# A build-time scheduler gets a longer latency for small transfers behind weight loads, and two margins

## The chip, the cores and the metric

One core of one Trainium2 chip. The metric is device time in microseconds (us), the median of several executions of the same program on the same data. Executions of one kernel agree here within 0.1% mostly. All runs told below are in the fast state, at a granted TensorE clock of 1.0 (0.999 in a few). Engines: PE is TensorE, ACT ScalarE, DVE VectorE, POOL GpSimd, SP the engine that issues nearly all transfers. "The profile" is a hardware trace of one execution; its span is about 2 us shorter than the time (690.4 and 692.2 for the profiled execution of the kernel before).

## The reference, cut to what matters

```python
x = A_x                                   # [1, 2048, 512] bf16
xn = _layernorm(x)
return x + _A_ref(xn, A_wqkv, A_wo) + _B_ref(xn, B_w1, B_b1, B_w2, B_b2)

def _A_ref(x, wqkv, wo):                  # attention, 32 heads of 16, softmax over 2048 keys
    ...
    scores = jnp.einsum("bhqd,bhkd->bhqk", q, k) * scale
    p = _softmax(scores, axis=-1)
    o = jnp.einsum("bhqk,bhkd->bhqd", p, v)
    return ... @ wo

def _B_ref(x, w1, b1, w2, b2):            # a second layernorm, then an MLP over the 2048 tokens
    u = _gelu(jnp.einsum("bsd,sf->bdf", h, w1) + b1)      # F = 1376
    y = jnp.einsum("bdf,fs->bds", u, w2) + b2
```

The bulk is 32 x 2048 x 2048 exponentials. The kernel cuts them into 1024 tiles of 128 x 1024.

## The kernel before

It is one program with the order of every engine's instructions fixed at build time. A Python scheduler, inside the kernel file, keeps a clock for each engine, looks at what could be done next, and greedily appends the candidate with the earliest estimated time. Nothing at run time follows this clock: the chip keeps each engine's order and waits on semaphores. The time of a transfer in it:

```python
if op.is_dma:
    op.t0 = max(self.free[eng], ready)
    self.free[eng] = op.t0 + cost[0]      # DMA_I = 0.65: SP's issue
    op.t1 = op.t0 + cost[1]               # DMA_L = 3.0: landed
```

A candidate's estimate adds a slack of `DMA_SLACK = 0.8` us for each operand that a transfer writes. The slack only delays the moment at which the candidate is chosen; it is not in the clock.

```python
def est(specs, slack=0.0):
    for s_ in specs:
        r = max(r, sc.ready(s_["eng"], s_["reads"], s_["writes"], slack=slack, dma_slack=DMA_SLACK))
```

An exponential tile goes to ScalarE as one instruction, or to VectorE as one (`dexp`), followed by three shifted copies by VectorE or GpSimd. The first costs PE one group of four PV matmuls (softmax weights times V), the second four groups. Which engine takes a tile is the scheduler's choice, so the split (715 to 309 before) is a result of the order.

After each of the 32 blocks of heads the denominators go around by transfers, all issued by SP, and meet again in VectorE:

```python
for c in range(4):   # dcomp <- OT32      4 small transfers
...                  # oC32  <- OT32      8 small transfers
yield "dve", [... e.reciprocal(rcomp[:, eb, :], dcomp[:, eb, :]) ...]
...                  # rden_scratch <- rcomp
for r in range(4):   # denb <- rden_scratch   4 small transfers
...
for h in range(2):   # the products, for each second block
    yield "dve", [... e.tensor_tensor(oT(qb)[0:m, T, cs], oC32[...], denb[...], ALU.mult) ...]
```

The MLP runs in PE's gaps: eleven first-layer tiles, each with a 512 KB load of `w1` (the last 384 KB), then sixteen output tiles, each with a 320 KB load of `w2` and two small ones. These loads stand in SP's order among the small transfers above.

The softmax here doesn't subtract the row's maximum and nothing guards it: scores larger than these inputs give would overflow.

Of the kernel before, what the change touches and what calls it, by code (L numbers as in the profile page):

```python
# [28 lines left out]
NBLK = NQB * NG  # L29
NN = NBLK * NKT * 2  # L30
# [22 lines left out]
SEM = 0.05  # L53
PE_SWITCH = 0.10
PER_LIST = 16
LN2_AT = 12
PIECE_MIN = 6
PIECE_OPEN = 1
HOLD_MAX = 2.0
PE_LAT = 0.40  # L60
# [5 lines left out]
DMA_I = 0.65  # L66
DMA_L = 3.0
DMA_SLACK = 0.8
EXT_SLACK = 0.2
PV_SLACK = 0.1  # L70
GEN_SLACK = 0.0
# [2 lines left out]
OT_I, OT_L = 0.60, 0.685  # L74
D_END = 1022
D_FLY = 3
D_BACK = 0.5
D_STEAL = 0.3
D_LATE = 0.5
P_KEEP = 4  # L80
DEAD_SLACK = 0.1
PAIR_WAIT = 0.0
PORT_SLACK = 0.5
PE_FIT = 0.05
TABLE = 1.3
# [2 lines left out]
Q_GUARD = 8  # L88
KV_LEAD = 16
HARD_HOLD = 10  # L90
LATE_BY = 0
EX_FROM = 34
EX_RATE = 0.15
EX_EARLY = 10
# [28 lines left out]
class Sched:  # L123
    ENGS = ("pe", "act", "dve", "pool", "sp")

    def __init__(self, nc, es):
        self.nc = nc
        self.es = es
        self.streams = {e: [] for e in self.ENGS}
        self.order = []  # L130
        self.last_writer = {}
        self.readers = {}
        self.dma_ops = []
        self.free = {e: 0.0 for e in self.ENGS}
        self.busy = {e: 0.0 for e in self.ENGS}
        self.pe_mode = None
        self.pe_end = 0.0
        self.pe_tiles = {}
        self.phase = 0
        self.pieces = {}  # L140
        self.pe_log = []
        self.port_iv = {"dve": [], "pool": []}
        self.port_op = None

    def _deps(self, eng, reads, writes, dma):
        deps = set()
# [36 lines left out]
    def _time(self, op, cost, ready, port):  # L183
        eng = op.eng
        if port:
            ready = self.port_time(eng, max(self.free[eng], ready), cost[0])
        if op.is_dma:
            op.t0 = max(self.free[eng], ready)
            self.free[eng] = op.t0 + cost[0]
            op.t1 = op.t0 + cost[1]  # L190
        elif eng == "pe":
            mode, tiles, dur = cost
            t = max(self.free["pe"], ready)
            if mode != self.pe_mode:
                t = max(t, self.pe_end + PE_SWITCH)
                self.pe_mode = mode
                self.pe_tiles = {}
                self.phase += 1
            for x in tiles:
                t = max(t, self.pe_tiles.get(x, 0.0))  # L200
            for x in tiles:
                self.pe_tiles[x] = t + dur
            self.pe_end = max(self.pe_end, t + dur)
            self.free["pe"] = t + 0.004
            self.busy["pe"] += dur * len(tiles) / 4.0
            op.t0, op.t1 = t, t + dur + PE_LAT - 0.214
            self.pe_log.append((t, dur * len(tiles) / 4.0))
        else:
            op.t0 = max(self.free[eng], ready)
            self.free[eng] = op.t0 + cost[0]  # L210
            self.busy[eng] += cost[0]
            op.t1 = op.t0 + cost[1]
        if port:
            self.port_iv[eng] = self.port_iv[eng][-7:] + [(op.t0, op.t0 + cost[0])]
# [124 lines left out]
def bass_parallel_sum__softmax_full_mha__mixer_token_mlp__prompt_kernel(  # L339
# [18 lines left out]
    with ExitStack() as es:  # L358
# [31 lines left out]
        dcomp = sb("dcomp", [128, 2, 16], F32)  # L390
# [8 lines left out]
        def oT_keys(qb, T):  # L399
            return [("oTc", qb, T)] + (WKV_KEYS if qb >= 2 else [])  # L400
# [622 lines left out]
        def task_epilogue(b):  # L1023
            p, e_ = divmod(b, 2)
            qb, T = PAIRS[p]
            eb, tb_ = b % 2, p % 2
            yield "gate", lambda: b < 2 or b - 2 in ot_free
            yield "pvev", [dict(eng="dve", fn=lambda e: e.tensor_copy(OT32[:, eb, :], bank(PV_BANK)),  # L1028
                                reads=[("bank", PV_BANK)], writes=[("OT32", eb)])]
            for c in range(4):  # L1030
                yield "sp", [dict(dst=dcomp[32 * c:32 * c + 32, eb, :],
                                  src=OT32[32 * c + 16:32 * c + 17, eb, :].rearrange("o (c x) -> o c x", x=16),
                                  reads=[("OT32", eb)], writes=[("dcomp", eb, c)], name="den_in")]
            g_in = dict(gen=task_o_in(b), cur=None)
            if b == NBLK - 2:
                yield "call", lambda: (step_gen(g_in), frees.append(g_in))
            else:
                yield from task_o_in(b)
            yield "dve", [dict(eng="dve", fn=lambda e: e.reciprocal(rcomp[:, eb, :], dcomp[:, eb, :]),
                               reads=[("dcomp", eb, r) for r in range(4)], writes=[("rcomp", eb)], cost=(0.2, 0.25))]  # L1040
            yield "sp", [dict(dst=rden_d[eb].rearrange("(p x) -> p x", x=16), src=rcomp[:, eb, :],
                              reads=[("rcomp", eb)], writes=[("rden_d", eb)], name="den_mid")]
            for r in range(4):
                a, i = divmod(r, 2)
                ro = 64 * e_ + 16 * r
                src = rden_d[eb:eb + 1, :].rearrange("o (h i a x) -> o h i a x", h=2, i=2, a=2)[:, :, i, a, :]
                yield "sp", [dict(dst=denb[ro:ro + 16, tb_, :].rearrange("p (h x) -> p h x", h=2),
                                  src=src.to_broadcast([16, 2, 256]),
                                  reads=[("rden_d", eb)], writes=[("denb", tb_, e_, r)], name="den_out")]
            half = b == NBLK - 2  # L1050
            if e_ == 0 and not half:
                return
            es_ = (0,) if half else (0, 1)
            m = 64 if half else 128
            if half:
                yield "call", lambda: sc.add("dve", lambda e: e.memset(oT(qb)[64:128, T, :], 0.0),
                                             writes=oT_keys(qb, T), cost=(0.2, 0.26))
            yield "gate", lambda: b in ot_free and (half or b - 1 in ot_free)
            for h in range(2):
                cs = slice(256 * h, 256 * h + 256)  # L1060
                yield "dve", [dict(eng="dve", fn=lambda e, cs=cs: e.tensor_tensor(  # L1061
                    oT(qb)[0:m, T, cs], oC32[0:m, tb_, cs], denb[0:m, tb_, cs], ALU.mult),
                    reads=[("oC32", tb_, x, c, a) for x in es_ for c in range(4) for a in range(2)] +
                          [("denb", tb_, x, r) for x in es_ for r in range(4)],
                    writes=oT_keys(qb, T) + [("oTh", h)], port=True, cost=(0.33, 0.41))]
            yield "call", lambda: oT_done.add((qb, T))

        oT_done = set()
# [200 lines left out]
        def est(specs, slack=0.0):  # L1269
            s0 = specs[0]  # L1270
            r = 0.0
            for s_ in specs:
                r = max(r, sc.ready(s_["eng"], s_["reads"], s_["writes"], slack=slack, dma_slack=DMA_SLACK))
            t = max(sc.free[s0["eng"]], r)
            if s0.get("port"):
                t = sc.port_time(s0["eng"], t, s0["cost"][0])
            return t
# [24 lines left out]
        def pieces():  # L1302
# [12 lines left out]
            for tries in range(2):  # L1315
                for o in list(g["open"]):
                    for r in sorted(o[1]):
                        if piece_phase[1] not in (None, r) or max(sc.free["pe"], sc.pe_tiles.get(r, 0.0), sc.piece_ready(r)) + 0.214 > lim:
                            continue
                        sp_ = o[0](r, not g.get("begun"), hold and g["stop"] and len(g["open"]) == 1 and len(o[1]) == 1)  # L1320
                        if est(sp_) > sc.free["pe"] + 0.02:
                            continue
                        if not g.get("begun"):
                            g["begun"] = True
                            g["cur"] = ("pe", g["front"](False))
                        piece_phase[1] = r
                        for z in sp_:
                            add(z)
                        o[1].discard(r)
                        if not o[1]:  # L1330
                            g["open"].remove(o)
                        if hold and not g["open"]:
                            g.pop("since", None)
                            step_gen(g)
                            return
                        break
                if len(g["steps"]) >= PIECE_MIN and len(g["open"]) < PIECE_OPEN and g["steps"][-1][1]:
                    g["open"].append((g["steps"].pop(-1)[1], {0, 1, 2, 3}))
                else:
                    return  # L1340
# [22 lines left out]
        step_gen(g_h)  # L1363
        fin_next = 0
        while True:
            cands = []

            for g in sorted(frees, key=lambda g: not (g["cur"] and g["cur"][0] == "sp" and g["cur"][1][0]["name"] == "q_row")):
# [289 lines left out]
```

## Time and profile before

| | before |
|---|---|
| time, median of 4 | 691.96 us (691.90 to 692.06) |
| span of the profile | 690.4 us |
| exponential tiles on ScalarE / VectorE | 715 / 309 |
| last exponential on ScalarE ends at | 681.88 us |
| last PV matmul ends at | 682.22 us |

The busy shares, the waits and the rows of the groups are shown in the prediction. Timelines (columns): start, duration, engine, line, operation, tiles, form, count, and in brackets the idle time before and what ended it.

```profile
677.03 4.84 ACT L768 ACTIVATE pT<-ps 128x1024 bf16<-128x1024 f32 x5
687.32 0.60 ACT L1127 ACTIVATE oT<-ps 128x512 bf16<-128x512 f32 x1 [5.44 <-PE ps L1107]
...
666.33 0.82 PE L842 MATMUL ps<-gT_sb,wblk 128*32 128x512 bf16 x12
...
681.48 0.74 PE L811 MATMUL ps<-pT,V 128*32 128x256 bf16 x16
682.16 0.60 PE L1107 MATMUL ps<-wo_c,wkv_raw 128*128 128x512 bf16 x2
```

The exponentials end at 681.9 us, the PV matmuls 0.3 us later, and then comes a closing part (last denominators, last output rows) of 8.2 us, in which ScalarE sits idle for 5.44 us.

### The profile page before, as it was taken

The numbers are of one execution on the slowest core, as the hardware profiler recorded it, in microseconds if no ns is written. First come the engines' busy times: TensorE is split into PE (matmuls) and PEld (weight loads), VectorE is DVE, ScalarE is ACT, GpSimd is POOL, SyncE is SP. The second block draws the span as 40 slices with busy tenths as digits, with TensorE's granted clock in tenths as the row PEclk, the third lists the DMA queues.
The fourth block names the chain that finished last, engine by engine and source line by source line (L and its number), as shares of the span: only waits on it lengthen the run. The fifth ranks groups of instructions, "written<-read, shape, count | busy, mean of one in ns | idle before, by whom it ended". The sixth has DMA issues, their size and how long they took to land.

```text
span 690.4 us, 29398 instructions
## 1 busy us (share of the span) xinstructions
PE 674.3 (98%) x12934; PEld 309.7 (45%) x12934; DVE 618.7 (90%) x895; ACT 672.3 (97%) x734; POOL 401.7 (58%) x690
## 2 busy tenths in 40 slices
PE   7999999999999999999999999999999999999998
PEld 4534544435444454444444444444444444444444
DVE  7989899998889989889999989898998988888987
ACT  5999999999999999999999999999999999999995
POOL 4536557563455756656666576665665665654643
PEclk9999999999999999999999999999999999999999
DMA  7402001221002200022220212222221222313201
GB/s 214 101 5 54 21 18 21 50 45 29 19 18 50 48 20 19 23 52 49 49 42 20 58 29 55 53 55 55 49 49 34 58 53 57 70 28 87 47 22 48
DMA packets 85728, 32.32 MB, mean 47 GB/s; under 512 B 67424, under 2 KB 85600, under 8 KB 85600
## 3 DMA queue, kind: packets, MB, share of 16 engines
q1 hardware_dynamic: 85168, 30.05, 19.1%
q8 instruction: 101, 1.65, 1.1%
q10 hardware_dynamic: 432, 0.39, 0.2%
q14 instruction: 27, 0.22, 0.1%
HBM read 21.76 MB, written 2.35 MB: 35 GB/s over the span
## 4 chain that ended last, share of the span: by engine, by line
PE 78%; ACT 13%; DVE 5%; issue 1%; POOL 1%; SPq 0%; DMA 0%; DVEq 0%
PE ps L811 32%; PE ps L744 28%; PE ps L842 14%; ACT pT L768 10%; ACT x_sb L768 2%; PE ps L896 1%; DVE pT L779 1%; DVE OT L1028 1%; ACT gT_sb L953 1%; DVE hx L567 1%; DVE oT L1061 0%; SPq L436 0%; DMA denb<-rden_scratch 0%; POOL mv L563 0%; PE ps L648 0%
## 5 line engine op out<-in xcount | busy, mean ns | idle before, releaser
L768 ACT ACTIVATE pT<-ps 128x1024 bf16<-128x1024 f32 x535 | 521.1, 1126 | 2.7 <-PE ps L744 2.1
L779 DVE TENSOR_SCALAR pT<-ps 128x1024 int16<-128x1024 f32 x222 | 271.2, 1222 | 28.0 <-PE ps L744 21.2
L744 PE MATMUL ps<-QT,KT 32*128 32x512 bf16 x2048 | 283.1, 384 | 6.0 <-ACT pT L768 3.0
L785 POOL INT64_ADD pT<-pT x319 | 193.0, 613 | 117.1 <-DVE pT L788 77.5
L811 PE MATMUL ps<-pT,V 128*32 128x256 bf16 x4728 | 249.4, 276 | 3.5 <-DVE OT L1028 3.1
L768 ACT ACTIVATE x_sb<-ps 128x1024 bf16<-128x1024 f32 x180 | 194.0, 1130 | 0.6 <-PE ps L744 0.5
L744 PEld LDWEIGHTS ps<-QT,KT 32*128 32x128 bf16 x2048 | 78.2, 91 | 183.7 <-ACT pT L768 69.8
L811 PEld LDWEIGHTS ps<-pT,V 128*32 128x32 bf16 x4728 | 110.3, 96 | 87.3 <-issue 68.8
L785 POOL INT64_ADD x_sb<-pT x142 | 86.6, 613 | 70.0 <-DVE pT L788 32.2
L811 PE MATMUL ps<-x_sb,V 128*32 128x256 bf16 x1840 | 116.4, 275 | 0.7 <-DVE OT L1028 0.4
L779 DVE TENSOR_SCALAR x_sb<-ps 128x1024 int16<-128x1024 f32 x87 | 106.3, 1221 | 8.8 <-PE ps L744 6.7
L785 POOL INT64_ADD pT<-x_sb x115 | 70.1, 618 | 45.7 <-DVE pT L788 27.9
L788 DVE TENSOR_SCALAR pT<-pT 128x1024 int16<-128x1024 int16 x148 | 62.9, 427 | 4.3
L811 PE MATMUL ps<-pT,VM 128*32 128x256 bf16 x888 | 61.6, 274 | 0.0
L842 PE MATMUL ps<-gT_sb,wblk 128*32 128x512 bf16 (+1 forms) x704 | 61.2, 383 | 0.0
L811 PEld LDWEIGHTS ps<-x_sb,V 128*32 128x32 bf16 x1840 | 46.4, 96 | 29.4 <-issue 23.4
L842 PE MATMUL ps<-hx,wblk 128*32 128x512 bf16 x598 | 52.2, 383 | 0.0
L785 POOL INT64_ADD x_sb<-x_sb x55 | 33.4, 612 | 21.7 <-DVE pT L788 11.9
L850 PE MATMUL ps<-hx,wblk 32*128 32x512 bf16 (+1 forms) x92 | 35.6, 387 | 0.0
L788 DVE TENSOR_SCALAR pT<-x_sb 128x1024 int16<-128x1024 int16 x65 | 27.3, 427 | 1.8
L811 PEld LDWEIGHTS ps<-pT,VM 128*32 128x32 bf16 x888 | 23.4, 96 | 9.5 <-issue 8.2
L788 DVE TENSOR_SCALAR x_sb<-pT 128x1024 int16<-128x1024 int16 x57 | 23.9, 420 | 1.5
(111 smaller groups left out, 449.1 us busy)
## 6 DMA issues: line engine op xcount, KB each, us to landing
wblk<-in_B_w_dram SPq DMA_DIRECT2D x10, 512.0 KB, 4.5
wblk<-in_B_w_dram SPq DMA_DIRECT2D x16, 320.0 KB, 3.5
oC<-OT SPq DMA_DIRECT2D x248, 16.0 KB, 1.8
denb<-rden_scratch SPq DMA_DIRECT2D x124, 32.0 KB, 2.3
xr<-in_A_x_dram SPq DMA_DIRECT2D x16, 128.0 KB, 3.5
dcomp<-OT SPq DMA_DIRECT2D x124, 2.0 KB, 1.7
QT<-Qall SPq DMA_DIRECT2D x120, 16.0 KB, 1.8
out_dram<-osb SPq DMA_DIRECT2D x14, 128.0 KB, 2.0
```

Of the source, the lines that this page charges most:

```text
L567: return [dict(eng="dve", fn=lambda e: e.tensor_scalar(xn_sb[:, t, :], xn_sb[:, t, :], mv[:, t, 3:4], None, ALU.mult), reads=[("xn", t), ( ...
L744: specs.append(dict(eng="pe", fn=lambda e, r=r, bk=bk: e.matmul(bank(bk), lhsT=KT[32 * r:32 * r + 32, T, 128 * kt:128 * (kt + 1)], rhs=QT[ ...
L768: return [dict(eng="act", fn=lambda e: e.activation(buf(pbuf[n]), ps[:, s_ * 1024:(s_ + 1) * 1024], ACTF.Exp, scale=LN2_128), reads=[("ban ...
L779: return dict(eng="dve", fn=lambda e: e.tensor_scalar(buf_i(w), ps[:, s_ * 1024:(s_ + 1) * 1024], IBIAS, 0.0, ALU.add, ALU.max), reads=[(" ...
L785: return dict(eng=eng, fn=lambda e: e.int64_add(buf_i(o).bitcast(I64), buf_i(w).bitcast(I64), SHIFTS[k] * 0x0001000100010001), reads=[("pT ...
L788: return dict(eng=eng, fn=lambda e: e.tensor_scalar(buf_i(o), buf_i(w), float(SHIFTS[k]), 1.0, ALU.add, ALU.mult), reads=[("pT", w)], writ ...
L811: specs.append(dict(eng="pe", fn=lambda e, c=c, h=h, i=i, off=off: e.matmul(bank(PV_BANK)[32 * c:32 * c + 32, 256 * par:256 * par + 256], ...
L842: specs.append(dict(eng="pe", fn=lambda e, c=c, w=w: e.matmul(bank(EX_BANK)[32 * c:32 * c + w, :], lhsT=lhs_of(32 * c, 32 * c + w), rhs=rh ...
L850: return [dict(eng="pe", fn=lambda e: e.matmul(bank(EX_BANK)[0:dst_rows, :], lhsT=lhs_of(0, dst_rows)[rs], rhs=rhs[rs], start=begin, stop= ...
L896: return [dict(eng="pe", fn=lambda e, ct=ct, c=c: e.matmul(bank(EX_BANK)[32 * c:32 * c + 32, 128 * i:128 * (i + 1)], lhsT=xnT[:, ct, 128 * ...
L953: yield "act", [dict(eng="act", fn=lambda e, ap=ap: e.activation(ap, ap, ACTF.Gelu_apprx_tanh), reads=[("gT", f) for f in fts], writes=[(" ...
L1028: yield "pvev", [dict(eng="dve", fn=lambda e: e.tensor_copy(OT32[:, eb, :], bank(PV_BANK)), reads=[("bank", PV_BANK)], writes=[("OT32", eb)])]
```

## The change

Its intent is to bring the scheduler's clock nearer to the chip: a small transfer just behind a weight load lands late, so VectorE should not be sent to wait for it. Two of the instructions that read such transfers get larger slacks. A table of rules for six other constants comes in with it, with all 128 entries on rule 0.

```diff
+SEG = 8
+RULES = (
+    (0.5, 0.5, 0.3, 0.0, 6, 0),
     ... nine more rows, not selected
+RULE_OF = "000 ... 000"          # 128 zeros
+DMA_SLACK_RCP = 1.5
+DMA_SLACK_OT = 2.5
+DMA_BIG = 5.2
-D_BACK = 0.5
-D_STEAL = 0.3
-D_LATE = 0.5
-PAIR_WAIT = 0.0
-PIECE_MIN = 6
-LATE_BY = 0
@@ a transfer's time
-            op.t1 = op.t0 + cost[1]
+            op.t1 = op.t0 + max(cost[1], DMA_BIG - (op.t0 - self.big))
+            if op.name in ("ld_w1", "ld_w2a"):
+                self.big = op.t0
@@ reciprocal
+    dma_slack=DMA_SLACK if b >= NBLK - 4 else DMA_SLACK_RCP
@@ products
+    dma_slack=DMA_SLACK if b >= NBLK - 4 else DMA_SLACK_OT
@@ est
-    ... dma_slack=DMA_SLACK
+    ... dma_slack=s_.get("dma_slack", DMA_SLACK)
@@ at each step
+    D_LATE, D_BACK, D_STEAL, PAIR_WAIT, piece_min, LATE_BY = RULES[int(RULE_OF[min(next_n, NN - 1) // SEG])]
```

More of the change, by code (lines that the diff above doesn't have):

```diff
@@ L55 @@
 PER_LIST = 16
+SEG = 8
+RULES = (
+    (0.5, 0.5, 0.3, 0.0, 6, 0),
+    (0.3, 0.5, 0.3, 0.0, 6, 0),
+    (0.8, 0.5, 0.3, 0.0, 4, 0),
+    (0.5, 0.8, 0.3, 0.0, 6, 0),
+    (0.5, 0.5, 0.45, 0.15, 6, 0),
+    (0.5, 0.5, 0.15, 0.0, 4, 0),
+    (0.5, 0.35, 0.3, 0.3, 4, 0),
+    (0.8, 0.8, 0.3, 0.0, 99, 0),
+    (0.5, 0.5, 0.3, 0.0, 4, 6),
+    (0.5, 0.8, 0.45, 0.1, 4, -6),
+)
+RULE_OF = "00000000000000000000000000000000000000000000000000000000000000000000000000000000000000000000000000000000000000000000000000000000"
 LN2_AT = 12
-PIECE_MIN = 6
 PIECE_OPEN = 1
@@ L143, in __init__ @@
         self.port_op = None
+        self.big = -9.0
     def _deps(self, eng, reads, writes, dma):
@@ L1039, in task_epilogue @@
             yield "dve", [dict(eng="dve", fn=lambda e: e.reciprocal(rcomp[:, eb, :], dcomp[:, eb, :]),
-                               reads=[("dcomp", eb, r) for r in range(4)], writes=[("rcomp", eb)], cost=(0.2, 0.25))]
+                               reads=[("dcomp", eb, r) for r in range(4)], writes=[("rcomp", eb)], cost=(0.2, 0.25), dma_slack=DMA_SLACK if b >= NBLK - 4 else DMA_SLACK_RCP)]
             yield "sp", [dict(dst=rden_d[eb].rearrange("(p x) -> p x", x=16), src=rcomp[:, eb, :],
@@ L1064, in task_epilogue @@
                           [("denb", tb_, x, r) for x in es_ for r in range(4)],
-                    writes=oT_keys(qb, T) + [("oTh", h)], port=True, cost=(0.33, 0.41))]
+                    writes=oT_keys(qb, T) + [("oTh", h)], port=True, cost=(0.33, 0.41),
+                                   dma_slack=DMA_SLACK if b >= NBLK - 4 else DMA_SLACK_OT)]
             yield "call", lambda: oT_done.add((qb, T))
@@ L1272, in est @@
             for s_ in specs:
-                r = max(r, sc.ready(s_["eng"], s_["reads"], s_["writes"], slack=slack, dma_slack=DMA_SLACK))
+                r = max(r, sc.ready(s_["eng"], s_["reads"], s_["writes"], slack=slack, dma_slack=s_.get("dma_slack", DMA_SLACK)))
             t = max(sc.free[s0["eng"]], r)
@@ L1336, in pieces @@
                         break
-                if len(g["steps"]) >= PIECE_MIN and len(g["open"]) < PIECE_OPEN and g["steps"][-1][1]:
+                if len(g["steps"]) >= piece_min and len(g["open"]) < PIECE_OPEN and g["steps"][-1][1]:
                     g["open"].append((g["steps"].pop(-1)[1], {0, 1, 2, 3}))
```

## The prediction

> **What bounds the kernel now.** I read the page first (busy shares, slices), then the busy time of the engines in one long middle stretch, then ScalarE's and VectorE's waits, then the two lines that the change touches, and last the DMA issues around a weight load. The page:
>
> ```profile
> span 690.4 us, 29398 instructions
> PE 674.3 (98%) x12934; PEld 309.7 (45%) x12934; DVE 618.7 (90%) x895; ACT 672.3 (97%) x734; POOL 401.7 (58%) x690
> ...
> ACT  5999999999999999999999999999999999999995
> ```
>
> Three engines look full, but only one has no hole. ScalarE is at nine tenths in every slice but the first and the last. The stretch from 60 to 670 us says the same more sharply (columns: PE, PEld, DVE, ACT, POOL busy):
>
> ```profile
> 60.00:670.00 610.00, 603.11 (x11940) 275.34 (x11936) 551.80 (x743) 608.53 (x663) 364.40 (x606) 1.00 0.19 42
> ```
>
> ScalarE is busy for 608.5 of 610 us, VectorE for 551.8, so 58 us of VectorE are spare there. The groups of the whole run and ScalarE's waits:
>
> ```profile
> L768 ACT ACTIVATE pT<-ps 128x1024 bf16<-128x1024 f32 x535 | 521.1, 1126 | 2.7 <-PE ps L744 2.1
> L768 ACT ACTIVATE x_sb<-ps 128x1024 bf16<-128x1024 f32 x180 | 194.0, 1130 | 0.6 <-PE ps L744 0.5
> ...
> L779 DVE TENSOR_SCALAR pT<-ps 128x1024 int16<-128x1024 f32 x222 | 271.2, 1222 | 28.0 <-PE ps L744 21.2
> L779 DVE TENSOR_SCALAR x_sb<-ps 128x1024 int16<-128x1024 f32 x87 | 106.3, 1221 | 8.8 <-PE ps L744 6.7
> ```
>
> 1024 exponential tiles are shared: 535 + 180 = 715 on ScalarE, 222 + 87 = 309 on VectorE. Starts of neighbouring exponentials on ScalarE lie 904 ns apart (median of the trace), from 12.5 to 681.9 us. 715 x 0.904 = 646 us, and the rest of those 669 us is the GELU with its two table loads (about 8 us), small delays of 10 to 100 ns, and a few waits. ScalarE waits for scores only 2.6 us in the whole run. So **the length of the run is, to first order, the number of exponentials that the build-time schedule gives to ScalarE, times 0.92 us**: (608.5 - 8.0) / 655 = 0.917 us each in the stretch above.
>
> The chain of waits puts 78% on PE and only 13% on ScalarE. I do not take this as "PE is the bound": the chain steps from a score to the engine that freed its PSUM bank and back, and the three banks' pairs turn around just in time. It does say that PE has little reserve.
>
> **What the Trainium skill says.** "Perfetto Trace Analysis", section "Identifying the Most-Contended Engine": occupancy is a fair measure for Scalar and Vector, matmul busy time is not. I follow it, and treat ScalarE's 97% as meaning more than PE's 98%; the trace agrees in so far as ScalarE has no idle slice in the middle. "DMA: Bandwidth & Descriptors", section "Queues, rings and completion order": on each DMA engine the descriptors of one queue are consumed in ring order, so a small transfer issued just behind a large one on the same queue has to follow it. The trace agrees: all these transfers are issued by SP, and the landing times below show it. "SBUF — State Buffer", section "Who interferes with whom": a VectorE instruction with two SBUF inputs contends with GpSimd's reads. The trace fits: four products take 742 or 743 ns instead of 424, each with a GpSimd add under way. The change's margins are no cure for that.
>
> **The change part by part.**
>
> Part 1, the table of rules. The string has 128 zeros, one for each 8 of the 1024 tiles, so the first row is in force everywhere: 0.5, 0.5, 0.3, 0.0, 6, 0. These are the values of the constants that were deleted. It removes and adds nothing: 0 us.
>
> Part 2, DMA_BIG. A DMA issued t us after a weight load is now modelled to land at 5.2 - t instead of 3.0, where that is more, so only those within 2.2 us of one are touched. The trace backs the figure. For the reciprocal broadcasts (denb), issue to landing is 4.24 us in the median (largest 5.56) for the 8 with a known landing that start under 1 us behind a load, 3.37 for the 16 between 1 and 2.2 us, and 1.87 for the 59 more than 4 us behind one. The old model's 3.0 plus its slack 0.8 covers all but the first class. No DMA is added, removed or resized. The medians that the page lists for these transfers:
>
> ```profile
> wblk<-in_B_w_dram SPq DMA_DIRECT2D x10, 512.0 KB, 4.5
> ...
> denb<-rden_scratch SPq DMA_DIRECT2D x124, 32.0 KB, 2.3
> dcomp<-OT SPq DMA_DIRECT2D x124, 2.0 KB, 1.7
> ```
>
> Part 3, reciprocals, margin 0.8 to 1.5 us. Between the last dcomp issue and the reciprocal the generator puts eight oC copies, 8 x 0.65 = 5.2 us of SP in the model. The reciprocal's new earliest time is 3.05 + 1.5 = 4.55 us after that issue, still under 5.2; so it moves only behind a weight load (5.2 + 1.55 = 6.75, up to 1.5 us later). And there is nothing to win:
>
> ```profile
> L1039 DVE RECIPROCAL rcomp<-dcomp x31: 236/243/246, 59.8 to 674.8; 128x16 f32<-128x16 f32 x31
> ```
>
> Under it the view of idle time lists no wait at all for these 31. Value 0 us.
>
> Part 4, products (oT), margin 0.8 to 2.5 us, for 14 of the 16 pairs. Each slips by 1.7 us in VectorE's order, about one exponential with one shift (1.13 + 0.335 in the model). This is where the waits are:
>
> ```profile
> L1061 DVE TENSOR_TENSOR wkv_raw<-oC,denb 128x256 bf16<-128x256 f32 x14 | 7.2, 514 | 1.0 <-issue 0.8
> L1061 DVE TENSOR_TENSOR oT<-oC,denb 128x256 bf16<-128x256 f32 x16 | 7.2, 448 | 3.8 <-DMA denb<-rden_scratch 2.1 <-issue 1.3
> ```
>
> Of 4.8 us idle before the products, 2.1 are waits for denb, three times: 0.34 us at 133.2, 0.49 at 215.5, 1.25 at 298.7. Each follows a 512 KB load by about 5 to 6 us, with the landing at the very end of the gap. The largest, in VectorE's timeline:
>
> ```profile
> 296.65 0.76 DVE L788 TENSOR_SCALAR pT<-x_sb 128x1024 int16<-128x1024 int16 x2
> 298.66 0.88 DVE L1061 TENSOR_TENSOR oT<-oC,denb 128x256 bf16<-128x256 f32 x2 [1.25 <-DMA denb<-rden_scratch]
> 299.46 1.22 DVE L779 TENSOR_SCALAR pT<-ps 128x1024 int16<-128x1024 f32 x1
> ```
>
> Gaps of 0.34 to 0.49 us put down to "issue", at other products, have their denb long landed; a margin leaves them. The second half of the run (320 KB loads) has no denb wait at all. So the change can take away 2.1 us of VectorE idle time, all of it before 300 us.
>
> What is that worth at the end? Two ways. **(a) What ScalarE sees**: its spacing stretches by 0.52 us just after the product at 298.7 (a wait of 0.33 us among it), by 0.21 us next to the one at 133.2, and not at the third: 0.7 us. **(b) If VectorE's time is turned into exponentials**: VectorE has 610 - 90 (all its other work in the stretch) = 520 us for 296 tiles, 1.76 us each; ScalarE 0.917. Saving s on VectorE shortens the run by (s/1.76) / (1/0.917 + 1/1.76) = 0.34 s, so 2.1 us give 0.7 us. Both are **0.7 us, 0.1%**, and not to be added: (b) needs a re-deal that the model makes only by chance, as the model does not know these waits.
>
> Part 5, the re-deal. The schedule is greedy; every shifted product changes which engine takes the next tile and which PE job fits next. Each tile that moves from ScalarE to VectorE is worth about 0.9 us while VectorE has room, each one back costs it. The margins do not add work in the model, so I expect no drift, but a scatter: plus or minus 2 to 3 tiles of 309 (1%), my guess, makes 2 to 3 us. I give it a small favour of 0.5 us, as later products leave VectorE free for exponentials at moments when it stood waiting. Sum: 692.0 - 0.7 - 0.5 = 690.8 us.
>
> **The rivals.** *First, nothing to see:* VectorE has 58 us spare and catches up after each wait; ScalarE's 2.6 us of waits support this. Then 691.5 to 692.2. *Second, the re-deal dominates:* ScalarE's count becomes, say, 709 or 721 and the time goes by 5 us either way, 686.5 or 697.5. For it: the profile shows the time tied to this count. Against: only 14 product pairs and a few dozen modelled landings move. *Third, a new wait:* later products let oT and the buffer of oC be free later, and the output tasks that read oT, or GpSimd's adds that queue behind a product on the shared port, start later. GpSimd already waits 6.6 + 3.5 us for products, at 58% busy; it can stand that. A pair slips 1.7 us and pairs lie 40 us apart, so I give this at most +1 us. *Fourth, PE is the true bound*, as the chain suggests: then more tiles on VectorE (each brings three more groups of PV matmuls) win nothing, and the change stays within 0.5 us of 692.
>
> **Range and chances.** Centre 690.8; the direct gain can only lie between 0 and some 2 us; the scatter is the wide part, with a standard deviation of about 2.4 us, so 8 in 10 lie within about 3.1 us: 687.6 to 693.8. The 2% limits are 13.8 us away, over five such deviations; I leave 2% for each side for what I have not seen.
>
> **What would show each step right or wrong.** Right: the row of products shows no wait for denb (2.1 us now); reciprocals still show none; instruction counts of DMA are equal (124, 124, 248); ScalarE stays at 97% or more, and the change of time is about 0.92 us times the change of its 715. Wrong: denb waits remain, or appear before another line; ScalarE's waits for scores grow beyond 2.6 us; the count stays at 715 and the time moves by over 2 us, which would mean that spacing, the start or the tail made the difference; or the count moves by over 5.

## The result, and the profile after

The changed kernel takes 691.29 us (median of 4, 691.28 to 691.34), against 691.96. Ratios here are the mean time of one kernel's fast runs over that of the other's of the same rounds, so not quite the ratio of the medians: 0.999, 95% interval 0.9973 to 1.0008. All four runs of the one lie below all four of the other, by over 0.5 us. The result is correct.

The page of the changed kernel (its source lines are some 14 higher, so L782 is the L768 of before and L793 the L779):

```profile
span 689.5 us, 29510 instructions
PE 674.6 (98%) x12969; PEld 311.0 (45%) x12969; DVE 622.2 (90%) x896; ACT 669.5 (97%) x731; POOL 408.5 (59%) x701
...
L782 ACT ACTIVATE pT<-ps 128x1024 bf16<-128x1024 f32 x512 | 501.5, 1119 | 3.2 <-PE ps L758 2.5
...
L782 ACT ACTIVATE x_sb<-ps 128x1024 bf16<-128x1024 f32 x200 | 214.5, 1126 | 0.5 <-PE ps L758 0.4
```

ScalarE has 512 + 200 = 712 exponentials, three fewer; VectorE has 312. The stretch from 60 to 670 us, to set beside the same row of before:

```profile
60.00:670.00 610.00, 604.66 (x11992) 276.89 (x11984) 557.35 (x744) 608.59 (x663) 374.12 (x622) 1.00 0.19 42
```

ScalarE is as full as it was (608.59 to 608.53), VectorE and GpSimd do more. The products and the reciprocals in the groups, with the idle time before them last:

```profile
L1075 DVE TENSOR_TENSOR wkv_raw<-oC,denb 128x256 bf16<-128x256 f32 x14 | 7.5, 539 | 1.0 <-issue 0.8
L1075 DVE TENSOR_TENSOR oT<-oC,denb 128x256 bf16<-128x256 f32 x16 | 7.5, 467 | 2.0 <-issue 1.8
L1053 DVE RECIPROCAL rcomp<-dcomp 128x16 f32<-128x16 f32 x30 | 7.3, 243 | 0.0
```

The wait for denb (2.1 us of it before, as the profile puts it) is gone; what is left is the part put down to "issue". VectorE's timeline around the product that stood still for 1.25 us before:

```profile
298.17 0.43 DVE L802 TENSOR_SCALAR x_sb<-pT 128x1024 int16<-128x1024 int16 x1
298.67 1.23 DVE L793 TENSOR_SCALAR x_sb<-ps 128x1024 int16<-128x1024 f32 x1
299.81 0.41 DVE L1075 TENSOR_TENSOR oT<-oC,denb 128x256 bf16<-128x256 f32 x1
```

An exponential has taken the place in front of it. The gain is smaller than three tiles would make it, and the end of the run shows where the rest went:

```profile
678.45 1.07 ACT L782 ACTIVATE x_sb<-ps 128x1024 bf16<-128x1024 f32 x1
686.40 0.60 ACT L1142 ACTIVATE oT<-ps 128x512 bf16<-128x512 f32 x1 [6.89 <-PE ps L1122]
...
678.62 0.39 PE L856 MATMUL ps<-gT_sb,wblk 128*32 128x512 bf16 x4
679.05 0.39 PE L856 MATMUL ps<-xr,ident 128*32 128x512 bf16 x4
680.36 0.94 PE L825 MATMUL ps<-pT,V 128*32 128x256 bf16 x28
```

The last exponential ends at 679.52 us, 2.36 us earlier than before. But at 678.6 us PE still does MLP work of the sixteenth output tile; in the kernel before, the last such matmul (of the row at 666.33 above) started at 666.8 us. After the last exponential PE has 64 PV matmuls to do, where it had 4. They end at 681.51 us, 0.71 us earlier than before; the span is 0.9 us shorter, the time by the medians 0.67: the profiled execution of before took 692.20 us, 0.24 above its median.

### The profile page after: what moved, and what is told of

The parts are those of the page before. It is cut to its first block, busy times and chain, and to the rows that moved or that the text cites. A ratio compares the mean times of both kernels' runs of the same rounds, so it can differ in the third digit from the quotient of the medians.

```text
span 689.5 us, 29510 instructions
## 1 busy us (share of the span) xinstructions
PE 674.6 (98%) x12969; PEld 311.0 (45%) x12969; DVE 622.2 (90%) x896; ACT 669.5 (97%) x731; POOL 408.5 (59%) x701
## 4 chain that ended last, share of the span: by engine, by line
PE 67%; ACT 26%; DVE 4%; issue 2%; POOL 1%; DVEq 0%
PE ps L825 27%; PE ps L758 24%; ACT pT L782 17%; PE ps L856 12%; ACT x_sb L782 8%; PE ps L910 1%; DVE pT L793 1%; ACT gT_sb L967 1%; DVE hx L581 1%; DVE OT L1042 1%; POOL mv L577 0%; PE ps L662 0%; DVE oT L1075 0%; DVE x_sb L793 0%; PE ps L593 0%
## 5 line engine op out<-in xcount | busy, mean ns | idle before, releaser
L782 ACT ACTIVATE pT<-ps 128x1024 bf16<-128x1024 f32 x512 | 501.5, 1119 | 3.2 <-PE ps L758 2.5
L793 DVE TENSOR_SCALAR pT<-ps 128x1024 int16<-128x1024 f32 x229 | 279.6, 1221 | 23.6 <-PE ps L758 16.5
L799 POOL INT64_ADD pT<-pT x339 | 205.6, 615 | 116.1 <-DVE pT L802 67.5
L825 PE MATMUL ps<-pT,V 128*32 128x256 bf16 x4728 | 245.0, 275 | 1.8 <-DVE OT L1042 1.3
L782 ACT ACTIVATE x_sb<-ps 128x1024 bf16<-128x1024 f32 x200 | 214.5, 1126 | 0.5 <-PE ps L758 0.4
L799 POOL INT64_ADD x_sb<-pT x134 | 81.8, 613 | 68.1 <-DVE pT L802 31.9
L793 DVE TENSOR_SCALAR x_sb<-ps 128x1024 int16<-128x1024 f32 x83 | 101.3, 1221 | 9.0 <-PE ps L758 6.4
L799 POOL INT64_ADD x_sb<-x_sb x51 | 31.2, 615 | 17.4 <-DVE pT L802 10.7
L802 DVE TENSOR_SCALAR x_sb<-pT 128x1024 int16<-128x1024 int16 x65 | 27.7, 428 | 2.0
L802 DVE TENSOR_SCALAR pT<-x_sb 128x1024 int16<-128x1024 int16 x60 | 25.7, 429 | 1.5
```

The lines of the kernel that those rows point to most:

```text
L782: return [dict(eng="act", fn=lambda e: e.activation(buf(pbuf[n]), ps[:, s_ * 1024:(s_ + 1) * 1024], ACTF.Exp, scale=LN2_128), reads=[("ban ...
L793: return dict(eng="dve", fn=lambda e: e.tensor_scalar(buf_i(w), ps[:, s_ * 1024:(s_ + 1) * 1024], IBIAS, 0.0, ALU.add, ALU.max), reads=[(" ...
L799: return dict(eng=eng, fn=lambda e: e.int64_add(buf_i(o).bitcast(I64), buf_i(w).bitcast(I64), SHIFTS[k] * 0x0001000100010001), reads=[("pT ...
L802: return dict(eng=eng, fn=lambda e: e.tensor_scalar(buf_i(o), buf_i(w), float(SHIFTS[k]), 1.0, ALU.add, ALU.mult), reads=[("pT", w)], writ ...
L825: specs.append(dict(eng="pe", fn=lambda e, c=c, h=h, i=i, off=off: e.matmul(bank(PV_BANK)[32 * c:32 * c + 32, 256 * par:256 * par + 256], ...
```

## The experiments

**What needed no chip.** The program built from the change with DMA_BIG 0 and both slacks at 0.8 has, on every engine, the same instructions and waits in the same order as the kernel before (source line numbers aside): the table of rules with zeros does nothing. The reciprocal margin alone gives that same program too, and the change without that margin gives the changed kernel. So two of the four parts are without any effect, and only DMA_BIG and the product margin remain. They make four programs: before, after, and each part alone.

The scheduler's own clock can be printed at the end of a build: 677.3 us for before and 677.1 for after. This is arithmetic of the kernel's own model, not a time; "modelled end" means it below.

**Is it the waits, or the order?** In the first experiment the order stays and the waits go. The source of the 512 KB loads inside the loop (eight of the ten; the expectation says nine, which was a miscount) is one contiguous stretch, so they should land sooner. The data is then wrong; the check against the reference doesn't resolve this part of the sum.

```diff
+            if i >= NW and m == 128:
+                src = B_w1.rearrange("s f -> (s f)")[0:128 * 2048].rearrange("(p x) -> p x", x=2048)
+                dst = wblk[:, slot, :, :].rearrange("p st j -> p (st j)")
```

> The kernel before with every instruction in the same order and with the same waits; only the source of the nine full-width first-layer weight loads inside the loop is changed to one contiguous stretch of the same size (wrong result on purpose), so that they should land sooner and the small transfers behind them too. Theory W (the gain of the change comes from the three product waits for denb, 2.1 us of VectorE): the waits go and the time falls by 0.4 to 0.8 us, to about 691.3, as much as the change gained. Theory S (the gain comes from the other order and split of the work): the waits go and the time stays within 0.2 us of 691.96.

The loads of this run and its products (as L1061 before; the edit shifts lines by four):

```profile
wblk<-in_B_w_dram SPq DMA_DIRECT2D x10, 512.0 KB, 3.4
...
L1065 DVE TENSOR_TENSOR oT<-oC,denb 128x256 bf16<-128x256 f32 x16 | 7.8, 488 | 2.1 <-issue 1.6
```

The loads land in 3.4 us instead of 4.5, and no product is put down as waiting for denb. But only two of the three waits have gone: the idle time before these products falls by 1.7 us, not by 2.1, and the gap at 133 us stays, under another name (first line before, second line this run):

```profile
133.19 0.89 DVE L1061 TENSOR_TENSOR oT<-oC,denb 128x256 bf16<-128x256 f32 x2 [0.34 <-DMA denb<-rden_scratch]
...
133.28 0.88 DVE L1065 TENSOR_TENSOR oT<-oC,denb 128x256 bf16<-128x256 f32 x2 [0.34 <-issue]
```

The raw records of the trace (the views leave these out) show why. Before the first product of a pair VectorE's sequencer works through eight semaphore instructions (more or fewer at a few pairs), 98 ns apart. At 133 us none of the eight took more than 50 ns in either run, so none stood waiting for a landing. In the kernel before, the longest took 301 ns ahead of the product at 215.5 us and 1178 ns ahead of the one at 298.7; those two gaps fall from 0.49 and 1.25 us to under 0.01.

The time is 691.71 us (691.67 to 691.84) against 691.97 (691.87 to 692.46) in the same rounds, ratio 0.9996 (0.9983 to 1.0008). All five runs are below all nine of before, but by little: by the medians the waits cost **about 0.26 us**, between the two expectations. The two profiled executions lie 0.49 us apart. Over all rounds the executions of before fall into two groups, 691.83 to 692.07 and 692.17 to 692.46 us, and the profiled one is of the second; why there are two was not found.

The control has the same edit on the changed kernel.

> The same cheap weight loads in the changed kernel, whose products show no denb wait any more. Both theories: there is nothing left to take away, within 0.2 us of 691.29. If it gains as much as the kernel before does, the loads cost time by something else than the product waits.

It takes 691.31 us (the changed kernel: 691.29). There was nothing to take away, so the 0.26 us above belongs to the waits and not to the loads themselves.

**Each part alone.**

```diff
# ot_only                              # big_only
 DMA_SLACK_OT = 2.5                    -DMA_SLACK_OT = 2.5
-DMA_BIG = 5.2                         +DMA_SLACK_OT = 0.8
+DMA_BIG = 0.0                          DMA_BIG = 5.2
```

> Only the product margin (2.5 us); DMA_BIG at 0, reciprocal margin back at 0.8. Scheduled: 714 tiles on ScalarE, 310 on VectorE; its model ends at 678.8 us against 677.3 for before and 677.1 for after. Theory W: the product waits are gone or nearly so, thus about 691.3 like the full change. Theory S: the time follows the order that the scheduler happened on, about 1.5 us above before, 693.5.

> Only DMA_BIG = 5.2; both margins back at 0.8. Scheduled: 717 tiles on ScalarE, 307 on VectorE; the model ends at 681.6 us. Theory W: products behind a load wait less or not at all, so 691.3 to 692. Theory S: two tiles more on ScalarE and a worse end, 694 to 696.

The product margin alone takes 693.26 us, DMA_BIG alone 695.85: **1.3 and 3.9 us slower than before**, though the first has no denb wait in its profile, and the second has just one, of 1.1 us, after its last exponential. Theory W, that the gain comes from the waits, falls; the expectation from the order held for both. DMA_BIG alone has two tiles more on ScalarE, yet its last exponential ends at 681.99 us, almost as before (681.88). What makes it late is PE after that:

```profile
677.22 4.77 ACT L782 ACTIVATE pT<-ps 128x1024 bf16<-128x1024 f32 x5
690.96 0.60 ACT L1142 ACTIVATE oT<-ps 128x512 bf16<-128x512 f32 x1 [8.98 <-PE ps L1122]
...
681.21 1.25 PE L856 MATMUL ps<-gT_sb,wblk 128*32 128x512 bf16 x20
682.39 1.27 PE L864 MATMUL ps<-wo_c,wkv_raw 32*128 32x512 bf16 x3
683.60 0.40 PE L856 MATMUL ps<-xr,ident 128*32 128x512 bf16 x4
683.82 0.39 PE L825 MATMUL ps<-pT,V 128*32 128x256 bf16 x8
```

The last output tile runs until 684 us, in front of the last PV matmuls, and these end at 686.07.

**Which engine bounds?** Three runs make one engine's work smaller by a known piece and leave all orders alone (wrong results).

```diff
# before_act_short: from tile 64 on
-  buf(pbuf[n]), ps[:, s_ * 1024:(s_ + 1) * 1024]
+  buf(pbuf[n], 0, 1024 if n < 64 else 992), ps[:, s_ * 1024:(s_ + 1) * 1024 - (0 if n < 64 else 32)]
# before_pe_short: PV, output and moving operand
-  256 columns
+  240 columns
# before_dve_short
-  buf_i(w), ps[:, s_ * 1024:(s_ + 1) * 1024]
+  buf_i(w)[:, 0:992], ps[:, s_ * 1024:s_ * 1024 + 992]
```

> The kernel before, same instructions in the same order; from tile 64 on, ScalarE's exponentials cover 992 of their 1024 columns (wrong result on purpose). That is 32 columns at 0.83 ns, 27 ns for each of some 650 tiles, 17 us of ScalarE. Theory A (the prediction's: ScalarE bounds the run): 14 to 17 us less, 675 to 678. Theory P (TensorE is as full and sets the end): 0 to 4 us less. In between: both bound it in turn.

> The kernel before, same order; every PV matmul streams 240 of its 256 columns (wrong result on purpose). The scheduler reckons 0.107 us for four of them side by side, so 6.7 ns for each of 1951 such groups, 13 us of TensorE. Theory A: under 1.5 us less, as ScalarE goes on at its own pace and only the end after the last exponential gets a little shorter. Theory P: 8 to 13 us less, 679 to 684.

> The kernel before, same order; VectorE's exponentials cover 992 of 1024 columns (wrong result on purpose), 33 ns for each of 309, 10 us of VectorE. Both theories: VectorE has 58 us to spare, so under 1.5 us less. If it falls by over 4 us, VectorE is a bound after all.

Against 691.91 us in the same rounds: ScalarE's cut gives **8.1 us** (683.81), PE's 1.03 (690.88), VectorE's 0.53 (691.38). The cuts took hold: the starts of ScalarE's exponentials lie 878 ns apart in the median instead of 904, which is 26 ns x some 650 = 17 us; PV groups within runs of PV follow each other by 103 ns instead of 109 (medians), 6 ns x 1951 = 12 us. So ScalarE is the bound and PE and VectorE are not, but only half of ScalarE's cut comes out. Of 663 distances after 60 us, 115 now are over 60 ns longer than the median, where 44 were before, and these add up to 8.6 us more, about the half that is missing. ScalarE's groups, with its waits for scores:

```profile
L768 ACT ACTIVATE pT<-ps 128x992 bf16<-128x992 f32 (+1 forms) x535 | 499.6, 1014 | 4.5 <-PE ps L744 3.0 <-PE ps L850 0.4
L768 ACT ACTIVATE x_sb<-ps 128x992 bf16<-128x992 f32 (+1 forms) x180 | 177.0, 1013 | 1.4 <-PE ps L744 1.1
```

Its waits for scores grow from 2.6 to 4.5 us; the views do not name what else lengthens the distances. The likely reading is that the other engines are just behind: in this fixed order, built for the longer exponentials, a 3% faster ScalarE already meets them.

**Does the late output tile cost the end?** The changed kernel with the last output tiles due earlier:

```diff
-FIN_END = 985
+FIN_END = 960
```

> The changed kernel with the last output tiles due 25 tiles earlier (FIN_END 960 for 985), so that their matmuls should not lie behind the last exponential. 713 tiles on ScalarE, 311 on VectorE; its model ends 0.8 us before that of the changed kernel. If the late output tile is what the changed kernel loses at the end: about 1 to 1.5 us less than 691.29. If TensorE is full anyway and the work only changes places: within 0.8 us of it.

It takes 691.17 us, 0.12 less than the changed kernel. The last MLP matmul moves from 678.6 to 675.2 us and the last PV matmul ends 0.77 us earlier, at 680.74; but ScalarE has one tile more, and the closing part is 0.3 us longer. This is within the second expectation: the work changes places. PE still has 44 PV matmuls to do after the last exponential, so that the late output tile is what the changed kernel loses at the end is not shown.

**Other orders.** The table of rules lets one try many orders. I let a program change digits at random and keep what had an earlier modelled end, once with the new transfer model and once with the old one (DMA_BIG 0, both slacks 0.8), and ran a midway table and the last table of each.

```diff
-RULE_OF = "000 ... 000"
+RULE_OF = "000022000222200022000400401046333901030000000000000000000028114009000000211000022133110700070711114078883441446464
+           33255344420626"           # half_new, one string of 128 digits
```

> The changed kernel with another table of rules (128 digits found by trying tables and keeping those whose modelled end is earlier); 710 tiles on ScalarE, 314 on VectorE, modelled end 671.9 us against 677.1. So far measured time less modelled end is 14.66 for before, 14.19 for after, 14.46 with the product margin alone, 14.25 with DMA_BIG alone. Theory S (order and split, as the model has them, set the time): 671.9 + 14.2 = 686.1 us. Theory C (only ScalarE's count matters, 0.92 us each): two tiles fewer than after, 689.5. If the model's end is chance: about 691.

> The same kind of table, found by the same kind of trial, but with the scheduler's old DMA model (DMA_BIG 0, both margins 0.8): 710 and 314 tiles, modelled end 671.6 us. If the new DMA model is worth what the difference of the offsets says (0.2 to 0.5 us of waits that the old one does not know): 671.6 + 14.66 = 686.3 us with denb waits before products in the profile, so 0.2 slower than the other table in spite of the earlier modelled end. If it is worth nothing: 685.8.

> A table from midway through the trials, new DMA model: 709 and 315 tiles, modelled end 673.3 us. Theory S: 673.3 + 14.2 = 687.5. Theory C: 3 tiles fewer than after, 688.5.

> A table from midway, old DMA model: 711 and 313 tiles, modelled end 673.4 us. With the old offset 673.4 + 14.66 = 688.1; if the new DMA model is worth nothing 687.6. Theory C: 1 tile fewer than after, 690.4.

In the same rounds before takes 692.06 us. The four take 687.64, 687.69, **687.30** and 689.62 us, all correct. The best, half_new, is 4.8 us faster than before, ratio 0.9931 (0.9916 to 0.9946), and by the medians 4.0 us faster than the changed kernel, which did not run in these rounds: with the same transfer model and only another table of rules, it beats both. Its page:

```profile
span 685.4 us, 29587 instructions
PE 673.7 (98%) x13002; PEld 310.6 (45%) x13005; DVE 624.9 (91%) x895; ACT 666.1 (97%) x728; POOL 416.2 (61%) x714
```

The expectations from the modelled end held for half_new (687.5) and missed the others by 1.4 to 1.6 us: a table that is picked for an early modelled end gets part of it only on paper. The count alone (theory C: 689.5, 688.5 and 690.4) missed as well, by 0.8 to 1.9. All orders side by side (times in us; the last column is span less last PV matmul):

| kernel | time | ScalarE / VectorE tiles | modelled end | last exponential ends | last PV matmul ends | closing part |
|---|---|---|---|---|---|---|
| before | 691.96 | 715 / 309 | 677.3 | 681.88 | 682.22 | 8.2 |
| after | 691.29 | 712 / 312 | 677.1 | 679.52 | 681.51 | 8.0 |
| ot_only | 693.26 | 714 / 310 | 678.8 | 681.51 | 683.50 | 8.0 |
| big_only | 695.85 | 717 / 307 | 681.6 | 681.99 | 686.07 | 8.0 |
| after_fin960 | 691.17 | 713 / 311 | 676.3 | 679.30 | 680.74 | 8.3 |
| half_new | 687.30 | 709 / 315 | 673.3 | 675.29 | 677.45 | 8.0 |
| half_old | 689.62 | 711 / 313 | 673.4 | 677.59 | 679.12 | 8.7 |
| table_new | 687.64 | 710 / 314 | 671.9 | 676.78 | 677.14 | 8.7 |
| table_old | 687.69 | 710 / 314 | 671.6 | 676.39 | 677.22 | 8.3 |

## Why the prediction was right or wrong

**The range and the class were right** (691.29 in 687.6 to 693.8, within 2%), and the centre missed by 0.5 us. The sum came out better than its terms, by luck: in the profiled executions a last exponential 2.36 us earlier and an end 1.44 us longer happened to leave about what the waits and the small favour had been put at.

**Part 1, the table, 0 us, and part 3, the reciprocals, 0 us: right, exactly.** Both leave the program as it is.

**Part 4, the waits: right in kind, too large in size.** No DMA wait is left in the row of the products, and none takes its place elsewhere. Of 4.8 us idle before the products, 3.0 remain, put down to "issue", as the prediction said of such gaps. The waits were put at 0.7 us; with the order held, taking them away gave 0.26. Of the two terms of (a), 0.52 + 0.21 us, the second is wrong: the gap at 133 us was no wait for denb (see the first experiment), and ScalarE's stretch there stayed, 216 ns against 212. So only 1.7 of the 2.1 us could be taken away. The first term holds for the execution that was read: the stretch at 299.8 us vanished, and ScalarE, 0.1 us behind the kernel before until then, is 0.49 us ahead of it from 305 us to the end. By the medians it is 0.26, as the profiled execution of before, 692.20 us, lies 0.23 above the median of those rounds.

**Part 5, the re-deal: the step that failed.** It reads: "the length of the run is, to first order, the number of exponentials that the build-time schedule gives to ScalarE, times 0.92 us". ScalarE's count fell by three, worth 2.75 us, and its last exponential did end 2.36 us earlier. The time fell by 0.67. The step leaves out the stretch between the last exponential and the end, and so takes it for constant: it was 8.52 us before and is 9.96 after, in which PE works off 64 instead of 4 PV matmuls, and in DMA_BIG alone it is 12.05. In the table above the closing part after the last PV matmul is nearly constant (8.0 to 8.7 us); the count of ScalarE governs the first of two terms, PE's leftover the second. (At 0.917 us for each tile off 715, the count puts the last exponential to within 1.1 us, except in big_only, where it ends 1.7 us earlier than that.) So the prediction's "the change of time is about 0.92 us times the change of its 715" is wrong here, and it had no term for the end.

**The scatter was the larger force, and underrated for single parts.** The spread of 2.4 us was a guess. The two parts alone gave +1.3 and +3.9 us against before, and other tables up to -4.8. Of 29 builds, not run, with one constant of the transfer model moved a little (DMA_SLACK_OT, DMA_BIG or DMA_L), the modelled ends lie between 677.1 and 682.9 us, standard deviation 1.5, and the count on VectorE between 307 and 313. None is earlier than that of the change, 677.1. So these two values fit one another and this kernel; that they were chosen by such a trial is a guess. The small drift of 0.5 us in favour had no ground that the runs confirm.

**The rivals.** "Nothing to see" is rejected, but narrowly: the count moved and the end moved with it. "The re-deal dominates" is the one that held, for the mechanism: both single parts are slower in spite of fewer waits. The "new wait" did not come: GpSimd waits 6.5 us for products, less than the 11.2 before. "PE is the true bound" is rejected for the middle (PE's cut of some 12 us gave 1.03), and was right about the end, which it did not name.

**What stays open.** Is the new transfer model worth more than its own deal? Time less modelled end is smaller with it in all three pairs (14.2 against 14.7 us in after and before, 14.0 against 16.2 midway, 15.7 against 16.1 at the last tables). That points the right way, but of the denb waits that the profiles of the old tables name (0.3 us in table_old, 0.7 in half_old) only one in half_old, of 0.4 us at 676.2 us, is one; the others are again a gap of 0.34 us near 133 us with no semaphore instruction over 50 ns. The orders differ throughout, and three pairs, between 0.35 and 2.2 us apart, don't settle a size.

## What to carry to other kernels

When a greedy scheduler fixes the order, a change of one constant deals all cards anew: build each part alone, compare the programs before running them, and hold the order fixed when the question is what a wait costs. Here the engine that was full to 99% bounded the middle, with the others not far behind; read the end separately, for what another engine still has to do after the full one stops. Check a wait that the profile names against a run that removes its cause: one of three here was none. And once the model is nearly right, trying many deals (4.8 us here) can be worth more than mending one more wait (0.26 us).

## What the Trainium skill lacked or had wrong

- "DMA: Bandwidth & Descriptors", sections "Anatomy of one DMA — SWDGE (gpsimd) path" and "Queues, rings and completion order": they give a fixed cost of about 2 us, for transfers that GpSimd issues, and the ring order, but no figure for a small transfer behind a large one in one queue. In the trace before, the 32 KB broadcasts take 4.24 us (median of 8) when issued under 1 us behind a 320 or 512 KB load, 3.37 us (16) between 1 and 2.2 us, and 1.87 us (59) at over 4 us.
- "ScalarE: Activation LUTs", section "What ACT_TABLE_LOAD costs": 186 + 0.833 N ns less an overlap of 93 ns is 946 ns for N = 1024, an estimate from that page; the exponentials, which read PSUM, start 904 ns apart here. The section does not say for which memory its figure holds (elsewhere the skill does give ScalarE a smaller overhead on PSUM). The slope fits: 26 ns for 32 columns, 0.81 ns each.
- "Perfetto Trace Analysis", section "Identifying the Most-Contended Engine": optimising the engine with the highest occupancy is right here, but the page gives no warning of how soon the next one takes over: a cut of 17 us on ScalarE (97% busy) gave 8.1 us.
- No page that was read gives the cost of semaphore waits in front of an instruction (it would belong to "Perfetto Trace Analysis"). Eight of them, 98 ns apart, stand before the first product of most pairs; the usual distance from the first of them to the product is 0.75 us. Where VectorE's work in that time is shorter, a gap is left that the profile puts down to "issue": 0.34 us behind one shift of 0.43 us, none behind an exponential of 1.22 us (at 299.8 us after the change). This accounts for three of the six gaps after the change (0.34 and twice 0.46 us); two others (0.38 and 0.50 us) hold a further 0.37 us just ahead of the product, which stays open. No run tested it.
